# Storing a spectral layer's intermediates by even and odd frequency: fewer stores and loads, and some work moved

## The chip, the cores and the metric

The kernel runs on one core of a Trainium2 chip. Its time is the device time of one execution in microseconds (us), given as the median of several runs. A core has five engines that run side by side: TensorE (PE, matrix products), VectorE (DVE), ScalarE (ACT), GpSimd (POOL) and SyncE (SP). Here SP issues nearly all DMAs, the copies between DRAM and the core's memory. Each engine, and SP's issuing too, works through its own instructions in order; an instruction that has to wait holds back those behind it.

## The reference

The result is the sum of the input, a spectral filter of it, and a two-layer network on it:

```python
xn = layernorm(x)                      # x: 2048 x 512, rows normalised
A  = irfft2(rfft2(xn) * (w_r + 1j*w_i))   # over both axes
h  = xn @ w1 + b1                      # 512 -> 1792
B  = (h * tanh(softplus(h))) @ w2      # Mish, 1792 -> 512
return x + A + B
```

`x` is float32. Only 257 of the 512 columns of the spectrum are kept, since the input is real.

## The kernel before

All products run in float16 on TensorE. Each operand is split into a high and a low half, and a product is made of three matmuls (high by high, high by low, low by high), which gives nearly float32 accuracy. That makes `mm3`, lines 66 to 72, the commonest code on PE.

**The network.** The 2048 rows form four groups of 512 (`g`), the 1792 hidden columns 14 chunks of 128. `up(n)` makes one chunk of the hidden layer for one group (line 734, 12 matmuls of 128 x 512), `mish(n)`, `a_hi(n)` and `a_lo(n)` apply the activation and split it (ACT, ACT, DVE; lines 745, 754, 757), and `down(n)` adds the chunk's part to the output of its group (12 matmuls). Each `up` and each `down` is called a half tile. There are 56 of both, and they hardly depend on the spectral part, so they can be placed among its steps to keep PE busy.

**The spectral part.** The transform over the 2048 rows is done in two steps, as 128 x 16. In the first (`s1_mm`, `s1_mm_pair`), for each of 16 residues `s2`, the 128 rows of that residue are transformed. The result has 128 partitions: 64 first-axis frequencies by real and imaginary part. Residues of the last three groups are taken in pairs (`row_pair`): sums and differences of rows give even and odd frequencies apart, so that the partitions of such a tile come in the order all even, then all odd. For the first four residues the order is the natural one. `s1_out` copies the result out of the accumulator (ACT and DVE, lines 131 and 132) as float16 halves; `s1_store` or `s1_store_pair` writes it to the DRAM tensor `d_y1`. The latter spreads even and odd to alternate rows there, so `d_y1` has the natural order.

Then comes the second step, in four rounds `c` of 16 frequencies, each in four units: `load_yt` reads `d_y1` back with 128 partitions that mean something else (residue and slot), `p2_unit` transforms over the residues into the tile `z`, and `spectrum(c, par)` transforms over the columns (`dre` and `dim`, line 68), multiplies with the filter (DVE and POOL, with weights that `load_wx` brings: `wE`, `wO`) and splits the product into `u`. `par` is 0 for even columns, 1 for odd ones. A small detour for column 0 goes by two 2 KB DMAs (`er` and `es` to `g`) and back (`h` to `u`).

The way back mirrors this. `dp_unit` makes the inverse over the columns (`psA`, copied to `at`, lines 655 and 656), and four DMAs turn it to `ai` (line 662). `ip_pair` takes two units and makes the inverse over the residues (`psT`, line 678, copied to `tt`, lines 700 and 701) and stores it to the DRAM tensor `d_t` (line 707). There, too, even and odd frequencies are written apart, here as two halves of `d_t`. A pair has two tiles `tt`, each with two blocks of 64 partitions, each written as even and odd: eight stores. There are eight pairs. When all is stored, `load_yi` reads 16 tiles `yi` (line 865), each in two DMAs: even frequencies to partitions 0 to 63, odd to 64 to 127. Then `s1_inverse_pair` and `s1_inverse` make the last transform (`psY`), ACT copies it to `ys`, DVE adds it to the rows (`add_rows`, lines 896 to 898), and SP stores the output. The last sums of the network are added on DVE at line 844.

**What sets the order.** `opening` and `middle` are written out by hand and run as written: they hold the normalisation, the first transform of all rows, and the first 25 `up` and 20 `down`. `act_of(n)` is `up`, `mish`, `a_hi`, `a_lo`. `max_wm(c)` are reductions on DVE over the filter weights. After that the generator `stream_a` walks through the spectral steps and stops at each `yield`; at each stop the tuple `HALVES` says how many half tiles are put there: its first entry before the first `p2_unit`, its last ten before the ten inverse steps. Its entries add up to 67. There the framework's planner may still shift single instructions, but the first matmul of each step keeps its place in the order of the program. A few buffers tie the parts together: the two PSUM banks `ps_f` that all spectral products share, three buffers `q2` for `at` and `tt`, five buffers `big` for `yt`, `wE`, `wO` and others.

Of the kernel before, what the change touches and what calls it, by code (L numbers as in the profile page):

```python
# [11 lines left out]
F16 = mybir.dt.float16  # L12
# [7 lines left out]
P = 128  # L20
# [3 lines left out]
LAG = 2  # L24
LAST = 3
HALVES = (
# [4 lines left out]
)  # L31
NQ = 4
P2_AT, SP_AT = 0, 0
# [8 lines left out]
def spectral_mlp_kernel(ctx, tc, x, wt, w0, w1, b1, w2, cT, cIT, cM, out):  # L42
    nc = tc.nc
# [16 lines left out]
    outv = out.rearrange("(p s) d -> p s d", s=NS2)  # L60
    outw = out.rearrange("(h p s) d -> p s h d", h=2, s=NS2)

    d_y1 = dp.tile([64, P, 256], F16, tag="d_y1", name="d_y1")
    d_t = dp.tile([2, 2, 32, 2, 32, 256], F16, tag="d_t", name="d_t")

    def mm3(ps, stat, mov, start, stop, order=False):

# [20 lines left out]
    y1s = {}  # L88
# [46 lines left out]

    def s1_store(s2, n=2):
        k = s2 % 2 + 1
        nc.sync.dma_start(
            d_y1[4 * (s2 + 1 - n) : 4 * (s2 + 1)].rearrange("a p e -> p a e"),
            y1s[0][:, k - n : k].rearrange("p s a h e -> p (s a) (h e)"),  # L140
        )

    def s1_store_pair(s2):
        for t in range(2):
            nc.sync.dma_start(
                d_y1[4 * s2 : 4 * s2 + 8].rearrange("a (q t) e -> t q a e", t=2)[t],
                y1s[0][64 * t : 64 * t + 64].rearrange("p s a h e -> p (s a) (h e)"),
            )

    class Rows:  # L150
# [340 lines left out]
    def load_yt(c, b, n=1):  # L491
        t = big.tile([P, 2, 4, 2, P], F16, tag="big", name=f"yt_{c}_{b}")
        w = 2048 // n
        for k in range(n):
            o = (2 * c + b) * 2048 + k * w
            tc.keep_in_program_order(
                nc.sync.dma_start(
                    t.rearrange("p g a h e -> p (g a h e)")[:, k * w : (k + 1) * w],
                    d_y1.rearrange("a (c f) e -> (a c) (f e)", c=2)[:, o : o + w],
                )  # L500
            )
        yts.setdefault(c, []).extend([t[:, 0], t[:, 1]])
# [164 lines left out]
    def ip_pair(c, g):  # L667

        fgs = (4 * c + g, 4 * c + g + 1)
        ai = [ait.pop(fg) for fg in fgs]  # L670
        ps = [ps_f.tile([P, 4, P], F32, tag="f", name=f"psT_{fg}") for fg in fgs]
        tiles = [(u, r) for u in (1, 0) for r in (1, 0)]
        passes = ((0, 0), (0, 1), (1, 0))

        def quarter(u, r, k, v, ls):
            hc, hm = passes[k]
            qs = slice(64 * r, 64 * r + 64)
            return nc.tensor.matmul(  # L678
                ps[r][64 * u : 64 * u + 64, ls],
                c_ip2[qs, v, hc, :],  # L680
                ai[u][qs, ls, hm, :],
                start=k == 0,
                stop=k == 2,
            )

        def rest(k, u, r):
            return quarter(u, r, k, 0, slice(1 if fgs[u] == 0 else 0, 4))

        for k in range(3):
            for t in tiles:  # L690
                i = rest(k, *t)
                if (k, t) == (0, tiles[0]):
                    tc.keep_in_program_order(i)
        if fgs[0] == 0:
            for k in range(3):
                for r in range(2):
                    quarter(0, r, k, 1, slice(0, 1))
        for r in range(2):
            tt = tp.tile([P, 4, 2, P], F16, tag="q2", name=f"tt_{fgs[r]}", bufs=3)
            nc.scalar.mul(tt[:, :, 0, :], ps[r], 2.0**-12)  # L700
            nc.vector.scalar_tensor_tensor(  # L701
                tt[:, :, 1, :], ps[r], 2.0**-12, tt[:, :, 0, :], op0=ALU.mult, op1=ALU.subtract
            )
            for u in range(2):
                f = 2 * fgs[u]
                for t in range(2):
                    nc.sync.dma_start(  # L707
                        d_t[r, t, f : f + 2].rearrange("f c q e -> (c q) f e"),
                        tt[64 * u : 64 * u + 64].rearrange("p (f t) h e -> p t f (h e)", t=2)[:, t],
                    )  # L710


    macc, yacc = {}, {}
# [141 lines left out]
    def load_yi(todo):  # L855
        spots = []
        for tag in ("z", "u"):
            t = tp.tile([P, 4, 4, 2, P], F16, tag=tag, name=f"yi_{tag}")
            spots += [t[:, k] for k in range(4)]
        for k in range(4):  # L860
            t = tp.tile([P, 2, 4, 2, P], F16, tag=f"w{k}", name=f"yi_w{k}")
            spots += [t[:, 0], t[:, 1]]
        for s2, t in zip([4 * g + s + k for g, s, n in todo for k in range(n)], spots):
            for par in range(2):
                nc.sync.dma_start(
                    t[64 * par : 64 * par + 64].rearrange("p (r a) h e -> p r (a h e)", r=2),
                    d_t[:, par, :, :, 2 * s2 : 2 * s2 + 2].rearrange("r f c a e -> (f c) r (a e)"),
                )
            yis.append(t)

    def s1_inverse(g, s):
# [373 lines left out]
    def row_pair(r, j):  # L1245
        s2 = 4 * r.g + 2 * j
        ps = [s1_bank(s2 + k) for k in range(2)]
        s1_mm_pair(s2 // 2 - 2, r.eo[j], ps)
        for k in range(2):
            s1_out(s2 + k, ps[k])  # L1250
        s1_store_pair(s2)

    def act_of(n):
        up(n)
        mish(n)
        a_hi(n)
        a_lo(n)
# [5 lines left out]
    def middle(r, ps1):  # L1263
        load_ct(2)
        down(0)
        row_in(r, 0)
        x2 = load_rows(2)
        r.turn(0)
        s1_out(0, ps1[0])
        w2_part(2)  # L1270
        down(1)
        row_in(r, 1)
        r.turn(1)
        s1_out(1, ps1[1])
        s1_store(1)
        down(2)
        r.fold(0, FOLD)
        w2_part(3)
        down(3)
        row_in(r, 2)  # L1280
        r.turn(2)
        w2_part(4)
        down(4)
        row_in(r, 3)
        r.turn(3)
        down(5)
        row_pair(r, 0)
        r.fold(1, FOLD)
        w2_part(5)
        down(6)  # L1290
        q = Rows(2, x2)
        q.stats(0)
        q.stats(1)
        w2_part(6)
        down(7)
        q.stats(2)
        q.stats(3)
        down(8)
        r1, r = r, q
        nc.sync.dma_start(cMt, cM)  # L1300
        x3 = load_rows(3, "u")
        load_ct(3)
        act_of(14)
        row_pair(r1, 1)
        for s in range(4):
            r.aggr(s)
        r.root()
        down(9)
        load_res(0)
        row_in(r, 0)  # L1310
        r.turn(0)
        act_of(15)
        row_in(r, 1)
        r.turn(1)
        down(10)
        r.fold(0, FOLD)
        act_of(16)
        row_in(r, 2)
        r.turn(2)
        load_wm(0)  # L1320
        load_wm(1)
        down(11)
        row_in(r, 3)
        r.turn(3)
        act_of(17)
        row_pair(r, 0)
        load_wm(2)
        load_w0()
        down(12)
        r.fold(1, FOLD)  # L1330
        q = Rows(3, x3)
        for s in range(4):
            q.stats(s)
        act_of(18)
        load_wm(3)
        load_wm(4)
        down(13)
        mlp_end(0)
        r2, r = r, q
        homes[19] = tp.tile([P, 2, 512], F16, tag="q2", name="a_q2", bufs=3)  # L1340
        act_of(19)
        row_pair(r2, 1)
        for s in range(4):
            r.aggr(s)
        r.root()
        down(14)
        row_in(r, 0)
        r.turn(0)
        max_wm(0)
        act_of(20)  # L1350
        row_in(r, 1)
        r.turn(1)
        turn_w0()
        max_wm(1)
        down(15)
        r.fold(0, FOLD)
        load_wm(5)
        act_of(21)
        row_in(r, 2)
        r.turn(2)  # L1360
        down(16)
        row_in(r, 3)
        r.turn(3)
        load_wm(6)
        act_of(22)
        row_pair(r, 0)
        r.fold(1, FOLD)
        max_wm(2)
        down(17)
        max_wm(3)  # L1370
        load_wm(7)
        act_of(23)
        down(18)
        row_pair(r, 1)
        max_wm(4)
        max_wm(5)
        max_wm(8)
        act_of(24)
        max_wm(6)
        max_wm(7)  # L1380
        sum_wm()
        down(19)
        scale_wm()
        return 25, 20
# [28 lines left out]
def _dft_constants():  # L1413
# [8 lines left out]
    IT = T.reshape(128, 16, 128).transpose(2, 1, 0)  # L1422
    IT = IT.reshape(2, 32, 2, 16, 128).transpose(2, 1, 0, 3, 4).reshape(128, 16, 128)
    TW = T[:64, 4:].reshape(64, 6, 2, 2, 32, 2).transpose(2, 0, 1, 5, 3, 4).reshape(128, 6, 2, 64)
    T = T[:, :4].reshape(128, 4, 128)

    s = np.arange(16)
    a16 = 2 * np.pi * (np.outer(s, s) % 16) / 16
# [54 lines left out]

def _spectral_layout(wr, wi):

    f1 = np.arange(64)[:, None]
    j = _J[None]
    fp = np.where(f1 == 0, np.where(j < 8, 128 * j, 64 + 128 * (j - 8)), f1 + 128 * j)
    fm = (-fp) % 2048
# [51 lines left out]
```

## Time and profile before

| | us |
|---|---|
| median of 3 runs | 372.81 (371.75 to 373.81) |
| the profiled execution's own time | 371.67 |
| its span in the profile | 369.9 |
| PE busy | 355.4 |
| DVE busy | 279.6 |
| ACT busy | 188.6 |
| POOL busy | 48.3 |

The span runs from the first to the last recorded piece of work; the time of an execution has a little more around it. "Busy" is the time in which an engine has an instruction in work. Register, semaphore and DMA-issuing instructions do not count. Matmuls overlap: one of 128 x 512 is shown with 0.38 us while they follow one another every 0.22 us, so that busy times of single groups add up to more than the time they take. The rows of SP (`SPq`) show the issuing of a DMA; the transfer itself comes after, and its time to landing is listed apart. A row's value in brackets is the idle time of the engine just before it, with what ended the wait.

### The profile page before, as it was taken

Reading aid. Unit: us, or ns where it says so; the run is one execution under the profiler, and the core shown is the slowest. Engines: PE = TensorE matmul, PEld = TensorE weight load, DVE = VectorE, ACT = ScalarE, POOL = GpSimd, SP = SyncE. Lnnn points to the kernel's source line nnn. Section 1 sums busy time; section 2 is a strip of 40 time slices with the busy share of each in tenths; the row PEclk is TensorE's granted clock in tenths of the full one; section 3 lists DMA queues with packets and bytes.
Section 4 is the critical chain, followed back from the end, with each engine's and each line's share of the span. In section 5 each row is a group of like instructions: output and inputs, shape, how many; then the busy total and the mean of one; then the engine's idle time right before and its main releaser. Section 6 shows DMA issues by size and latency. Waiting matters only on the chain.

```text
span 369.9 us, 6245 instructions
## 1 busy us (share of the span) xinstructions
PE 355.4 (96%) x2283; PEld 174.3 (47%) x2283; DVE 279.6 (76%) x543; ACT 188.6 (51%) x288; POOL 48.3 (13%) x49
## 2 busy tenths in 40 slices
PE   7999999999999999999999999999989998979993
PEld 2544444444444445445554455445544543434453
DVE  4898998895788793789898747995399632249796
ACT  5989966545726623434446345445443543345421
POOL 0020002302206200302123003020212000000000
PEclk9999999999999999999999999999999999999998
DMA  8935944599786657048012536226833344466757
GB/s 274 316 126 189 217 110 92 117 225 250 178 252 148 164 132 277 2 114 289 12 30 64 128 60 207 65 80 138 244 82 100 66 103 96 89 183 202 186 121 221
DMA packets 61438, 54.98 MB, mean 149 GB/s; under 512 B 17456, under 2 KB 50512, under 8 KB 61280
## 3 DMA queue, kind: packets, MB, share of 16 engines
q1 hardware_dynamic: 60928, 54.06, 54.5%
q10 hardware_dynamic: 480, 0.52, 0.6%
q8 instruction: 18, 0.29, 0.3%
q14 instruction: 12, 0.10, 0.1%
HBM read 34.61 MB, written 12.58 MB: 128 GB/s over the span
## 4 chain that ended last, share of the span: by engine, by line
PE 73%; DVE 11%; DMA 6%; SPq 5%; ACT 2%; issue 2%; DVEq 0%; ACTq 0%
PE ph L734 33%; PE pa L68 10%; PE pa L72 10%; PE pa L71 10%; SPq L707 4%; DVE m L896 1%; DMA g<-es 1%; PE psS L108 1%; PE psT L678 1%; DVE at L656 1%; DMA ai<-at 1%; PE psP L522 1%; DMA x<-in_x_dram 1%; PE psP L532 1%; DMA g<-er 1%
## 5 line engine op out<-in xcount | busy, mean ns | idle before, releaser
L734 PE MATMUL ph<-xnT,w1t 128*128 128x512 f16 x672 | 153.6, 379 | 0.0
L734 PEld LDWEIGHTS <-w1t 128*128 128x128 f16 x672 | 64.7, 98 | 77.5 <-issue 2.5
L745 ACT ACTIVATE hb<-ph,b1t,fp_exp 128x512 f32<-128x512 f32 x56 | 43.2, 771 | 64.1 <-PE ph L734 64.1
L68 PE MATMUL pa<-w2t,a 128*128 128x512 f16 x181 | 68.7, 380 | 0.0
L72 PE MATMUL pa<-w2t,a 128*128 128x512 f16 x181 | 68.6, 379 | 0.0
L71 PE MATMUL pa<-w2t,a 128*128 128x512 f16 x181 | 68.6, 379 | 0.0
L757 DVE SCALAR_TENSOR_TENSOR a<-hb,ip_a,a 128x512 f16<-128x512 f32 x46 | 34.3, 748 | 31.5 <-ACT a L754 31.4
L754 ACT ACTIVATE a<-hb,ip_a 128x512 f16<-128x512 f32 x46 | 33.1, 720 | 2.3 <-DVE ip_a L294 1.2
L68 PEld LDWEIGHTS <-a 128*128 128x128 f16 x190 | 18.6, 98 | 21.3 <-issue 2.4
L72 PEld LDWEIGHTS <-a 128*128 128x128 f16 x190 | 18.6, 98 | 20.9
L71 PEld LDWEIGHTS <-a 128*128 128x128 f16 x190 | 18.6, 98 | 18.7
L255 POOL TENSOR_TENSOR xh<-xs,xh 128x512 f16<-128x512 f32 x12 | 15.4, 1294 | 56.7 <-ACT xh L229 37.4
L430 ACT ACTIVATE u<-w,sc_u 128x512 f16<-128x512 f32 x16 | 10.8, 715 | 18.0 <-DVE w L631 8.5
L701 DVE SCALAR_TENSOR_TENSOR tt<-psT,tt 128x512 f16<-128x512 f32 x16 | 10.5, 684 | 10.7 <-ACT tt L700 10.7
L537 DVE SCALAR_TENSOR_TENSOR z<-psP,z 128x512 f16<-128x512 f32 x16 | 10.8, 689 | 10.3 <-ACT z L536 10.3
L229 ACT ACTIVATE xh<-x,nb,rs 128x512 f16<-128x512 f32 x12 | 9.6, 805 | 12.2 <-DVE nb L223 7.3
L606 POOL TENSOR_TENSOR w<-X,wE 128x512 f32<-128x512 f32 x4 | 5.9, 1464 | 73.8 <-DMA wE<-in_wt_dram 45.6
L655 ACT ACTIVATE at<-psA 128x512 f16<-128x512 f32 x16 | 9.2, 588 | 11.3 <-PE psA L72 8.8
L700 ACT ACTIVATE tt<-psT 128x512 f16<-128x512 f32 x16 | 8.9, 587 | 11.8 <-PE psT L678 7.4
L162 DVE BATCH_NORM_STATS2 st<-x 128x6 f32<-128x512 f32 x16 | 10.3, 678 | 4.5 <-DMA x<-in_x_dram 4.5
L536 ACT ACTIVATE z<-psP 128x512 f16<-128x512 f32 x16 | 9.5, 595 | 7.1 <-PE psP L532 7.0
L431 DVE SCALAR_TENSOR_TENSOR u<-w,sc_u,u 128x512 f16<-128x512 f32 x16 | 11.3, 744 | 1.7 <-ACT u L430 1.7
(220 smaller groups left out, 578.2 us busy)
## 6 DMA issues: line engine op xcount, KB each, us to landing
wm<-in_wt_dram SPq DMA_DIRECT2D x8, 512.0 KB
ai<-at SPq DMA_DIRECT2D x64, 64.0 KB, 2.2
d_t<-tt SPq DMA_DIRECT2D x64, 64.0 KB, 2.1
w1s<-in_w_dram SPq DMA_DIRECT2D x7, 512.0 KB, 7.2
w2s<-in_w_dram SPq DMA_DIRECT2D x7, 512.0 KB, 3.2
x<-in_x_dram SPq DMA_DIRECT2D x12, 256.0 KB, 6.7
d_y<-y SPq DMA_DIRECT2D x12, 256.0 KB, 4.1
yt<-d_y SPq DMA_DIRECT2D x6, 512.0 KB
```

The costliest lines, as they stand in the source:

```text
L68: first = nc.tensor.matmul(ps, stat(0), mov(0), start=start, stop=False)
L71: nc.tensor.matmul(ps, stat(0), mov(1), start=False, stop=False)
L72: nc.tensor.matmul(ps, stat(1), mov(0), start=False, stop=stop)
L255: engine.tensor_sub(self.xh[s][:, 1, :], self.xs[s], self.xh[s][:, 0, :])
L430: nc.scalar.activation(dst_h, src, AF.Copy, scale=scale)
L431: nc.vector.scalar_tensor_tensor(dst_l, src, scale, dst_h, op0=ALU.mult, op1=ALU.subtract)
L537: nc.vector.scalar_tensor_tensor(zl, psv, 2.0**-14, zh, op0=ALU.mult, op1=ALU.subtract)
L707: nc.sync.dma_start(d_t[r, t, f : f + 2].rearrange("f c q e -> (c q) f e"), tt[64 * u : 64 * u + 64].rearrange("p (f t) h e -> p t f (h e) ...
L734: nc.tensor.matmul(ph[n + k], w1t[:, hw, dc, f * P : (f + 1) * P], xnT[g][:, hx, dc, :], start=(hw, hx, dc) == (0, 0, 0), stop=(hw, hx, dc ...
L745: nc.scalar.activation(hbt[n], ph.pop(n), AF.Mish, bias=b1t[:, f : f + 1], scale=s_exp[part_of(f)])
L754: nc.scalar.activation(act[n][:, 0, :], hbt[n], AF.Copy, scale=sc["a"])
L757: nc.vector.scalar_tensor_tensor(act[n][:, 1, :], hbt.pop(n), sc["a"], act[n][:, 0, :], op0=ALU.mult, op1=ALU.subtract)
```

## The change

The partition order "all even, then all odd" is now used for all tiles, from the first store to the last load:

- The constants for the first four residues (`T`) are permuted, so these tiles have it as well; the filter's layout (`f1` in `_spectral_layout`) is permuted to go with it.
- `d_y1` has even and odd frequencies as its outermost axis. Every store of `y` writes 64 partitions to 64 neighbouring rows. The first four residues take two stores for each two tiles, where they took one; the paired ones two, as before. `load_yt` reads one half or the other; pieces and sizes stay.
- In rounds 0 and 1 the second step now works on even frequencies, in rounds 2 and 3 on odd ones. So a block of 64 partitions of `tt` holds one kind only and is written by one store of 128 KB instead of two of 64 KB: four a pair instead of eight.
- A `yi` tile is loaded whole by one DMA of 256 KB instead of two of 128 KB.
- In `middle`, the last `row_pair` stands behind `act_of(24)` and `max_wm(4)` instead of ahead of them.
- `HALVES` has new entries, with the same number of them and the same sum.

The arithmetic, the number of matmuls and the bytes moved are the same.

```diff
 HALVES = (
-    2, 1, 0, 0, 1, 1, 1, 2, 0, 1, 1, 1, 2, 0, 0, 0, 0, 2, 0, 1, 0, 2, 0, 0, 1, 0, 1, 1, 0, 0, 1, 1,
-    0, 1, 1, 0, 0, 0, 0, 1, 0, 1, 0, 1, 0, 1, 1, 1, 1, 1, 0, 0, 0, 1, 0, 1, 1, 0, 0, 0, 0, 0, 1, 0,
-    0, 2, 0, 2, 0, 1, 1, 1, 0, 0, 1, 0, 1, 0, 0, 1, 1, 0, 0, 1, 1, 0, 0, 1, 1, 0, 4, 1, 1, 1, 3, 1,
-    2, 1, 1, 0,
+    3, 1, 0, 0, 0, 1, 0, 0, 0, 1, 1, 2, 1, 1, 2, 0, 1, 0, 2, 0, 0, 0, 0, 2, 1, 0, 1, 0, 1, 0, 0, 1,
+    2, 0, 1, 0, 0, 0, 0, 1, 1, 0, 2, 0, 0, 0, 1, 1, 0, 0, 0, 2, 0, 1, 1, 0, 1, 0, 0, 0, 0, 0, 1, 0,
+    1, 0, 1, 0, 2, 0, 2, 0, 1, 1, 1, 0, 0, 0, 1, 0, 2, 0, 0, 1, 1, 0, 1, 0, 0, 1, 3, 1, 1, 1, 1, 2,
+    2, 1, 1, 1,
 )
-    d_y1 = dp.tile([64, P, 256], F16, tag="d_y1", name="d_y1")
-    d_t = dp.tile([2, 2, 32, 2, 32, 256], F16, tag="d_t", name="d_t")
+    d_y1 = dp.tile([2, 64, 2, 32, 256], F16, tag="d_y1", name="d_y1")
+    d_t = dp.tile([2, 64, 2, 32, 256], F16, tag="d_t", name="d_t")
...
     def s1_store(s2, n=2):
         k = s2 % 2 + 1
-        nc.sync.dma_start(
-            d_y1[4 * (s2 + 1 - n) : 4 * (s2 + 1)].rearrange("a p e -> p a e"),
-            y1s[0][:, k - n : k].rearrange("p s a h e -> p (s a) (h e)"),
-        )
-
-    def s1_store_pair(s2):
         for t in range(2):
             nc.sync.dma_start(
-                d_y1[4 * s2 : 4 * s2 + 8].rearrange("a (q t) e -> t q a e", t=2)[t],
-                y1s[0][64 * t : 64 * t + 64].rearrange("p s a h e -> p (s a) (h e)"),
+                d_y1[t, 4 * (s2 + 1 - n) : 4 * (s2 + 1)].rearrange("a c q e -> (c q) a e"),
+                y1s[0][64 * t : 64 * t + 64, k - n : k].rearrange("p s a h e -> p (s a) (h e)"),
             )
...
-            o = (2 * c + b) * 2048 + k * w
+            o = (2 * c + b) % 4 * 2048 + k * w
...
-                    d_y1.rearrange("a (c f) e -> (a c) (f e)", c=2)[:, o : o + w],
+                    d_y1[(2 * c + b) // 4].rearrange("a c q e -> (a c) (q e)")[:, o : o + w],
...
             for u in range(2):
-                f = 2 * fgs[u]
-                for t in range(2):
-                    nc.sync.dma_start(
-                        d_t[r, t, f : f + 2].rearrange("f c q e -> (c q) f e"),
-                        tt[64 * u : 64 * u + 64].rearrange("p (f t) h e -> p t f (h e)", t=2)[:, t],
-                    )
+                f = 4 * fgs[u]
+                nc.sync.dma_start(
+                    d_t[r, f : f + 4].rearrange("f c q e -> (c q) f e"),
+                    tt[64 * u : 64 * u + 64].rearrange("p f h e -> p f (h e)"),
+                )
...
-            for par in range(2):
-                nc.sync.dma_start(
-                    t[64 * par : 64 * par + 64].rearrange("p (r a) h e -> p r (a h e)", r=2),
-                    d_t[:, par, :, :, 2 * s2 : 2 * s2 + 2].rearrange("r f c a e -> (f c) r (a e)"),
-                )
+            nc.sync.dma_start(
+                t.rearrange("p (r a) h e -> p r (a h e)", r=2),
+                d_t[:, :, :, 2 * s2 : 2 * s2 + 2].rearrange("r f c a e -> (f c) r (a e)"),
+            )
...
     def row_pair(r, j):
...
-        s1_store_pair(s2)
+        s1_store(s2 + 1)
...
         down(18)
+        max_wm(4)
+        act_of(24)
         row_pair(r, 1)
-        max_wm(4)
         max_wm(5)
         max_wm(8)
-        act_of(24)
         max_wm(6)
...
-    T = T[:, :4].reshape(128, 4, 128)
+    T = T[:, :4].reshape(128, 4, 2, 32, 2).transpose(0, 1, 4, 2, 3).reshape(128, 4, 128)
...
-    f1 = np.arange(64)[:, None]
+    f1 = np.arange(64).reshape(32, 2).T.reshape(64, 1)
```

## The prediction

> **What bounds the kernel now.** I read first the busy time by stretch, to see where TensorE (PE) is not full, since PE work is the same before and after. Columns: stretch, its length, busy us (count) of PE, weight loads, VectorE (DVE), ScalarE (ACT), POOL, PE clock, DMA share, GB/s.
>
> ```profile
> 0.00:20.00 20.00, 17.51 (x103) 8.97 (x104) 13.96 (x35) 15.48 (x24) 2.04 (x9) 1.00 0.86 278
> 20.00:230.00 210.00, 210.00 (x1285) 101.85 (x1283) 170.88 (x335) 116.05 (x177) 37.65 (x34) 1.00 0.56 148
> 230.00:240.00 10.00, 9.21 (x53) 4.46 (x51) 9.59 (x20) 4.75 (x8) 0.05 (x1) 1.00 0.22 61
> 270.00:280.00 10.00, 8.37 (x48) 4.03 (x46) 9.81 (x19) 4.02 (x6) 0.00 (x0) 1.00 0.25 65
> 290.00:330.00 40.00, 36.22 (x244) 17.36 (x243) 12.19 (x19) 15.67 (x24) 0.00 (x0) 1.00 0.44 102
> 360.00:369.90 9.90, 4.12 (x43) 3.34 (x41) 6.25 (x15) 1.37 (x2) 0.00 (x0) 0.87 0.75 219
> ```
>
> PE is full from 20 to 230 us. What a change of the spectral part can win is 0.79 us (230 to 240), 1.63 (270 to 280) and 3.78 (290 to 330), together 6.20, and some of the last 9.9 us. The clock is 1.00 in all of it. The waits of PE name what it lacked:
>
> ```profile
> PE psY L108 <- DMA yi_z<-d_t: 2.2, 3, 1.3
> PE dim L68 <- DVE at L656: 1.4, 2, 0.8
> PE psT L678 <- DMA ai<-at: 1.1, 1, 1.1
> ```
>
> Two of the three are DMAs issued by SP (SyncE). SP's own order of work shows why they are late (start, us, what):
>
> ```profile
> 305.74 5.10 SPq L662 DMA_DIRECT2D ai<-at  x8
> 310.94 10.71 SPq L707 DMA_DIRECT2D d_t<-tt  x16
> 322.57 5.27 SPq L865 DMA_DIRECT2D yi_z<-d_t  x8
> ```
>
> From 305.74 to 327.84 SP issues without a pause: 32 DMAs, 0.65 to 0.67 us apart. DMA engines are at a 0.44 share over 290 to 330. So the number of issues, not bytes, sets this stretch: `ai` of the last pair leaves behind stores of an earlier one, and sixteen stores stand before the first load of the inverse transform.
>
> **The change, part by part.** *Issue count.* The price of an issue against its size, and issue to landing:
>
> ```profile
> L707 SPq DMA_DIRECT2D d_t<-tt x64: 574/605/1652, 206.1 to 321.0; - x64
> L145 SPq DMA_DIRECT2D d_y<-y x12: 581/621/1352, 72.0 to 133.5; - x12
> d_t<-tt SPq DMA_DIRECT2D x64, 64.0 KB, 2.1
> d_y<-y SPq DMA_DIRECT2D x12, 256.0 KB, 4.1
> yi_z<-d_t SPq DMA_DIRECT2D x8, 128.0 KB, 2.9
> yt<-d_y SPq DMA_DIRECT2D x4, 256.0 KB, 4.5
> ```
>
> A 64 KB store takes 605 ns to issue and a 256 KB one 621: size costs SP nothing. The `d_t` stores go from 64 of 64 KB to 32 of 128 KB (four a pair), the `yi` loads from 32 of 128 KB to 16 of 256 KB; the stores of the first four `y` tiles go from 2 to 4. At 0.65 us that takes 20.8 + 10.4 off SP and adds 1.3 near 44 and 63 us, where PE is full (20 to 230): zero, at most 1.3 if that cover went. Pieces stay 512 B for stores and 1 KB a row for `yi`. Landing is not shown for the new shapes: a 128 KB store lies between 2.1 and 4.1, I take 2.8 (nearer the smaller one by size); a 256 KB load of full rows lies between 2.9 and 4.5, I take 3.5. The `yt` loads keep size and piece; their rows only lie closer in DRAM: zero, hidden by the same full stretch.
>
> *The end of the spectral part (290 to 330).* Rows for the last pair, and the length of one half tile of PE cover (12 matmuls):
>
> ```profile
> 312.57 0.75 PE L678 MATMUL psT<-ai,cMt 64*64 64x512 f16 x8 [1.12 <-DMA ai<-at]
> 314.21 0.69 DVE L701 SCALAR_TENSOR_TENSOR tt<-psT,tt 128x512 f16<-128x512 f32 x1 [2.94 <-ACT tt L700]
> 327.61 0.81 PE L108 MATMUL psY<-yi_z,cITt 64*64 64x256 f16 x21 [0.40 <-DMA yi_z<-d_t]
> 240.29 2.59 PE ph L734 x12
> ```
>
> Before, from the end of `psT` (about 313.5) to the inverse getting its data (327.61) go 14.1 us. New: first `tt` half ready 1.4 later (314.21 + 0.69), its two stores until 2.7, two more until 4.0. The last is issued at 3.4, lands at 3.4 + 2.8 = 6.2; two `yi` loads, the second issued at 6.85, landed at 6.85 + 3.5 = 10.4. HALVES now leaves four half tiles between this `psT` and the first inverse instead of five: 4 x 2.59 = 10.4 us of PE work. The stall is thus about nil, 2.3 at the slow ends (3.4 + 4.1 + 0.65 + 4.5 = 12.65) and nil at the fast ones; I take 0.5. The eight stores of the pair before are now four, so `ai` leaves 2.6 us earlier, and the 1.12 goes. The other 0.5 of this stretch I leave with 0.3. Gain: 3.78 - 0.8 = 3.0, between 1.0 and 3.8.
>
> By the Trainium skill, SBUF — State Buffer, section on Door 1, a transfer on partitions 0 to 63 reaches 8 of 16 ports, and one on 128 reaches all; with its fixed 2 us and 27 GB/s a port (an estimate from that page) the 128 KB store and the full-row 256 KB load each land in 2.6 us. The stall would be nil by it and the gain 0.5 more. The 4.1 of the 256 KB store above is slower than the 3.2 that it would give, so the rows stay in the sum.
>
> *The middle (230 to 280).* Here PE waited for DVE to empty its banks, and DVE for DMAs:
>
> ```profile
> 228.69 0.42 DVE L578 TENSOR_TENSOR r<-g,c0t 4x256 f32<-4x256 f32 x1 [1.26 <-DMA g<-es]
> 257.14 5.17 SPq L707 DMA_DIRECT2D d_t<-tt  x8
> 262.36 0.59 SPq L506 DMA_DIRECT2D wE<-in_wt_dram  x1
> 263.54 0.67 SPq L572 DMA_DIRECT2D g<-es  x1
> 266.24 0.69 DVE L605 TENSOR_TENSOR w<-X,wE 128x512 f32<-128x512 f32 x1 [1.98 <-DMA wE<-in_wt_dram]
> ```
>
> Near 262 the `wE` load and the small `g` transfers stand directly behind eight stores; with four, they leave up to 2.6 earlier, more than the 1.63 that PE lost after. Near 221 it is the same eight stores, then three 512 KB loads, then `g`: with the loads gone earlier the 1.26 shrinks, and with it the 0.79. Against that, HALVES is rearranged. Adding up its entries, the count is equal again at the same points (4 at the first spectrum, 19 at the second half of the second, 25, 30, 34, 36, 41 after), but between them it differs: the two halves of the first spectrum have one half tile between them instead of four, those of the second five instead of six.
>
> ```profile
> 182.90:196.90 14.00, 14.00 (x102) 7.75 (x100) 13.67 (x25) 7.50 (x13) 2.94 (x2) 1.00 0.14 39
> ```
>
> In the second spectrum DVE was busy 13.67 of 14.0 us with PE just covered. One half less bares at most 2.59; as the first spectrum now gives DVE its work earlier, I take 0.5, and 0.6 in all other places. Gain: 2.42 - 1.1 = 1.3, between -1.0 and 2.4.
>
> *The moved pair (front).* The last `row_pair` goes behind one `act_of` and one `max_wm`, and HALVES starts with 3 for 2, so four half tiles still stand between its `psS` and the first use of `yt`.
>
> ```profile
> 130.07 0.85 PE L108 MATMUL psS<-eo,cTt 64*64 64x256 f16 x24
> 131.59 1.29 DVE L132 SCALAR_TENSOR_TENSOR y<-psS,y 128x512 f16<-128x512 f32 x2 [0.60 <-ACT y L131]
> 137.25 1.76 SPq L497 DMA_DIRECT2D yt<-d_y  x4
> 141.39 0.22 PE L522 MATMUL psP<-cMt,yt 128*128 128x128 f16 x1
> L745 ACT ACTIVATE hb<-ph,b1t,fp_exp 128x512 f32<-128x512 f32 x56 | 43.2, 771 | 64.1 <-PE ph L734 64.1
> L757 DVE SCALAR_TENSOR_TENSOR a<-hb,ip_a,a 128x512 f16<-128x512 f32 x46 | 34.3, 748 | 31.5 <-ACT a L754 31.4
> ```
>
> But its copies now queue behind that tile's Mish, cast and rest on ACT and DVE (771 ns, about as much again, 748), which start only where `psS` starts: DVE gets to `y` about 1.6 us after `psS` ends instead of 0.7, so its two stores, and the `yt` loads that wait behind them on SP, go about 1.0 later. The first loads left at 137.25 and their data was read near 141.3 with PE full, so the slack is unknown: the cost is between 0 and 1.5, I take 0.5, the middle.
>
> *The tail.* The last ten inverses come earlier among the half tiles (after 60, 62, 64 of them instead of 62, 63, 65).
>
> ```profile
> 329.70:366.40 36.70, 34.41 (x289) 18.11 (x287) 34.17 (x70) 13.35 (x20) 0.00 (x0) 1.00 0.68 185
> 363.90 0.22 PE L72 MATMUL pe<-w2t,a 128*128 128x128 f16 x1
> 365.98 0.34 DVE L844 SCALAR_TENSOR_TENSOR y<-pe,s_out,y 128x128 f32<-128x128 f32 x1
> ```
>
> DVE ends 2.2 us after PE, having been idle 2.5 of 36.7 us; fed earlier it can make up to 1.7 of that, but may also hold PE if inverses come faster than it adds them (six pairs). I take 0.5, between -0.5 and 1.7.
>
> *Sum.* 3.0 + 1.3 - 0.5 + 0.5 = 4.3 us. The profiled execution took 371.67 (span 369.9 and 1.77 around it): 367.4. The median of the runs, 372.81, lies 1.14 above it, so the forecast is 372.81 - 4.3 = 368.5.
>
> **The rivals.** *Issues are not what binds, bytes are:* all bytes stay, and fewer, larger transfers land later. The Trainium skill, DMA: Bandwidth & Descriptors, section Issuing engines are not separate DMA queues, speaks for this: issue time is "usually small relative to the DMA itself". Against it: the 0.65 us spacing whatever the size, and the 0.44 share. Then the end keeps its 3.78 and only the slow-landing bounds apply: gain 1.3 - 0.5 = 0.8, 372.0. Chance 0.18.
>
> *DVE becomes the bound of the last stretch:* 34.17 us of DVE work cannot begin before the first inverse and ends 2 us behind PE; if five pairs one half tile apart back up on DVE and hold the two banks of the next, the tail gives nothing and 1.5 of the end's gain goes back: 4.3 - 0.5 - 1.5 = 2.3, 370.5. For it: 34.17 of 36.7. Against: PE's remaining work is as long, and `ys` has two buffers. Chance 0.14.
>
> *Slower: the first spectrum's missing cover.* With one half tile instead of four between its halves, `dre` of the second needs banks that DVE must empty first. If DVE does that only behind the whole of the first half's work, the three missing half tiles are bared, 3 x 2.59 = 7.8; less the 4.3 it makes 372.81 + 3.5 = 376.3. It decides from 4.3 us bared on. For it: DVE is full in this part (13.67 of 14.0). Against: the emptying subtractions come first in the code, and the half tiles are returned after. Chance 0.08.
>
> **How the numbers follow.** Forecast 0.60, the rivals 0.18, 0.14, 0.08. About 0.5% (1.86 us) can be told from no change: faster is below 370.95, slower above 374.67. Forecast and the DVE rival lie below: 0.74; bytes: 0.18 same; cover: 0.08 slower. The terms' good ends together give 3.8 + 2.4 + 1.7 = 7.9, hardly all at once; I end the range at a gain of 6.8 (366.0), and above at 372.6, which takes in the bytes rival.
>
> **What would show it.** In the changed profile: 32 `d_t` stores and 16 `yi` loads at 0.6 us each; SP with pauses between 295 and 325; PE idle in the 40 us before the first inverse down from 3.78 to about 0.8; waits for `ai` gone; DVE not waiting for `wE` and `g` in the last two spectra; DVE's last instruction under 2 us behind PE's. The forecast is wrong if issue time grows with the store's size, if new idle time of PE stands between 140 and 230, or if the first `psP` waits for `yt` by more than 1.5.

## The result, and the profile after

| | before | changed |
|---|---|---|
| median, us | 373.23 (4 runs, 371.75 to 373.81) | 363.52 (4 runs, 363.37 to 363.65) |
| profiled execution's own time | 371.67 | 363.37 |
| its span | 369.9 | 361.6 |

The ratio is 0.9746, with a 95% interval of 0.9715 to 0.9776: 9.7 us faster. The forecast was 4.3, the fastest end of its range 366.0. The direction was right; the gain is more than double what was forecast and outside the range.

Busy time by stretch in the changed kernel (columns as before: stretch, length, PE, weight loads, DVE, ACT, POOL, PE clock, DMA share, GB/s):

```profile
0.00:20.00 20.00, 17.43 (x103) 8.93 (x104) 14.01 (x35) 15.53 (x24) 2.04 (x9) 1.00 0.87 278
20.00:230.00 210.00, 209.66 (x1274) 101.42 (x1273) 170.71 (x337) 115.20 (x176) 37.36 (x34) 1.00 0.58 148
230.00:240.00 10.00, 10.00 (x71) 5.27 (x73) 9.60 (x20) 5.15 (x9) 0.94 (x1) 1.00 0.19 54
270.00:280.00 10.00, 10.00 (x48) 4.58 (x47) 8.86 (x18) 3.19 (x5) 2.37 (x2) 1.00 0.17 47
290.00:330.00 40.00, 40.00 (x295) 18.70 (x293) 17.78 (x30) 18.60 (x29) 0.00 (x0) 1.00 0.61 163
```

PE is full from 230 to 330. All three holes of the kernel before (0.79, 1.63 and 3.78 us) are closed, and one of 0.34 is new, before 230. All waits of PE that are left, in its waits:

```profile
PE ps_w L1010 <- POOL eps L1034: 1.3, 1, 1.3
PE pt L257 <- ACT xh L184: 1.2, 2, 0.9
PE psP L516 <- DVE z L531: 0.3, 1, 0.3
```

The first two belong to the first 20 us. None is for a DMA. SP's order of work in the last spectral stretch now has pauses (start, us, what):

```profile
301.19 5.59 SPq L656 DMA_DIRECT2D ai<-at  x8
307.82 6.85 SPq L700 DMA_DIRECT2D d_t<-tt  x8
316.61 1.92 SPq L857 DMA_DIRECT2D yi_z<-d_t  x4
```

Before, 32 issues stood without a pause between 305.7 and 327.8. Now there is a pause of a microsecond before the stores and of about 2 before the first load, which waits for the last store to land.

**How much each stall was.** The 6.20 us that the prediction set as the most to be won between 230 and 330 is too little, because of how busy time is counted. Two neighbouring matmuls of the kernel before, from PE's timeline:

```profile
235.73 0.38 PE L72 MATMUL dre<-z,cMt 128*128 128x512 f16 x1
236.90 0.38 PE L68 MATMUL dim<-z,cMt 128*128 128x512 f16 x1 [0.79 <-DVE at L656]
```

They start 1.17 us apart, where undisturbed ones follow at 0.22: the stall cost 0.95, and the profile shows 0.79, since a matmul shown with 0.38 us still covers 0.16 of the hole behind it. Counted from start to start, the eight stalls of the kernel before come to 7.7 us: 2.9 in the middle (near 236 and 276) and 4.8 at the end (300 to 328). In the changed kernel 0.5 is left, so 7.2 us of stalls are gone. PE's last matmul starts at 356.61, before at 363.90: 7.3 earlier, which the stalls thus account for. From there to the end of the span go 5.0 us instead of 6.0. Together that is the 8.3 us between the two profiled executions (371.67 and 363.37). The other 1.4 us between the medians come from executions of the kernel before that were slower than its profiled one; `fill` below bears on the cause.

### The profile page after: what moved, and what is told of

Same layout as the page of the kernel before. It is cut to its first block, busy times and chain, and to the rows that moved or that the text cites. A ratio compares the mean times of both kernels' runs of the same rounds, so it can differ in the third digit from the quotient of the medians.

```text
span 361.6 us, 6167 instructions
## 1 busy us (share of the span) xinstructions
PE 353.9 (98%) x2283; PEld 174.0 (48%) x2283; DVE 278.5 (77%) x543; ACT 187.7 (52%) x288; POOL 47.8 (13%) x49
## 4 chain that ended last, share of the span: by engine, by line
PE 90%; DVE 6%; ACT 1%; DMA 1%; issue 0%; DVEq 0%
PE ph L727 39%; PE pa L68 13%; PE pa L71 12%; PE pa L72 12%; PE psT L672 2%; PE psS L108 1%; PE psY L108 1%; DMA x<-in_x_dram 1%; PE psA L68 1%; PE psA L71 1%; PE psA L72 1%; PE psP L516 1%; PE psP L526 1%; DVE u L425 1%; PE psP L519 1%; DVE xh L188 1%
## 5 line engine op out<-in xcount | busy, mean ns | idle before, releaser
L695 DVE SCALAR_TENSOR_TENSOR tt<-psT,tt 128x512 f16<-128x512 f32 x16 | 10.4, 683 | 7.3 <-ACT tt L694 7.3
L600 POOL TENSOR_TENSOR w<-X,wE 128x512 f32<-128x512 f32 x4 | 5.1, 1274 | 69.6 <-DVE X L593 69.6
L694 ACT ACTIVATE tt<-psT 128x512 f16<-128x512 f32 x16 | 8.8, 589 | 10.7 <-PE psT L672 8.8
```

Of the source, the lines that this page charges most:

```text
L695: nc.vector.scalar_tensor_tensor(tt[:, :, 1, :], ps[r], 2.0**-12, tt[:, :, 0, :], op0=ALU.mult, op1=ALU.subtract)
```

## The experiments

The theory was that SP's issues were what PE waited for ("issues"): removing 48 of them won the time, and the half tiles only had to go where the room was. The rivals were that the new places of the half tiles won it ("placing"), or that bytes and landings count, not the number of transfers ("bytes"). The runs were made in three groups, each with its own runs of the kernel before, to which the ratios refer: a median of 372.8 for `layout_only`, `sched_only`, `stores8` and `loads2`, 373.1 for `pool_queue`, `fill`, `after_unmoved` and `tail0`, 372.74 for `mid8`, `end8`, `end2` and `end2_tail0`.

**The layout alone.** `HALVES` and the place of `row_pair` go back to the old ones.

```diff
 HALVES = (
-    3, 1, 0, 0, 0, 1, ...
+    2, 1, 0, 0, 1, 1, ...
...
         down(18)
+        row_pair(r, 1)
         max_wm(4)
-        act_of(24)
-        row_pair(r, 1)
         max_wm(5)
         max_wm(8)
+        act_of(24)
```

> The changed kernel with HALVES and the place of the last row_pair as before: only the new layout, with 32 stores and 16 loads. Theory 'issues' (what was won is SP's issue time; the half tiles only had to be put where it leaves room): most of the 9.7 us, 365 to 368. Rival 'placing' (the half tiles' new places won it, whatever SP does): at most 2 us, 371 to 373.

Measured: 364.74 us (364.17 to 364.81), ratio 0.9778 (0.974 to 0.9817). So the layout wins 8.1 us, even with half tiles that were placed for the old one. "Placing" alone is out. PE keeps one wait in the spectral part:

```profile
PE psA L68 <- DVE tt L695: 0.6, 1, 0.6
```

The new places bring another 1.2: PE's last matmul starts 0.6 earlier than here (357.19 against 356.61), and the rest of the span behind it is 5.0 instead of 5.7.

**The places alone.** The kernel before with the new `HALVES` and the moved pair.

```diff
 HALVES = (
-    2, 1, 0, 0, 1, 1, ...
+    3, 1, 0, 0, 0, 1, ...
...
         down(18)
+        max_wm(4)
+        act_of(24)
         row_pair(r, 1)
-        max_wm(4)
         max_wm(5)
         max_wm(8)
-        act_of(24)
```

> The kernel before with the new HALVES and the moved row_pair: 64 stores and 32 loads as before. 'Issues': SP still issues without a pause from 300 to the first inverse, which now has four half tiles of cover instead of five, so a stall of PE of some 4 us or more there: 372 to 376. 'Placing': 364 to 367.

Measured: 370.9 us (370.5 to 372.12), ratio 0.9949 (0.9926 to 0.9971). Neither expectation was right: it is 1.9 faster, not slower. The stalls at the end did grow as "issues" had it, by 1.1 us in these two waits together:

```profile
PE psY L108 <- DMA yi_z<-d_t: 2.6, 2, 1.3
PE psT L678 <- DMA ai<-at: 1.8, 1, 1.8
```

But the waits for DVE in the middle shrank from 2.4 to 0.6, with all 64 stores still there, the 0.5 for `tt` is gone, and the stretch behind PE's last matmul went from 6.0 to 4.9; together that is more. So the middle's stalls have two cures: the layout alone ends them (`layout_only` shows none), and the new places alone end most of them.

**Eight stores again, same bytes.** In the changed kernel each 128 KB store of `d_t` is cut in two; the partitions, the pieces and the loads stay.

```diff
-                f = 4 * fgs[u]
-                nc.sync.dma_start(d_t[r, f : f + 4]..., tt[64 * u : 64 * u + 64]...)
+                for t in range(2):
+                    f = 4 * fgs[u] + 2 * t
+                    nc.sync.dma_start(d_t[r, f : f + 2]..., tt[64 * u : 64 * u + 64, 2 * t : 2 * t + 2]...)
```

> The changed kernel with every 128 KB store of d_t cut into two of 64 KB on the same 64 partitions: eight stores a pair, same bytes and same pieces, loads whole. 'Issues': PE idle before the first inverse returns, eight issues of 0.65 more stand on its way, 5 us less what is slack: 366 to 370. 'Bytes' (fewer transfers do not matter, the bytes do): 363.5 as the changed kernel.

Measured: 369.57 us (368.08 to 370.86), ratio 0.9908 (0.9876 to 0.9939): 6.0 of the 9.7 us are gone, with the same bytes, layout and order. "Bytes" is out. SP again issues sixteen stores in a row, and the first load leaves at 321.80, in the changed kernel at 316.61:

```profile
309.47 10.77 SPq L701 DMA_DIRECT2D d_t<-tt  x16
321.80 1.93 SPq L858 DMA_DIRECT2D yi_z<-d_t  x4
```

PE's waits at the end are back, and one of those in the middle:

```profile
PE psY L108 <- DMA yi_z<-d_t: 2.4, 2, 2.0
PE psT L672 <- DMA ai<-at: 0.9, 1, 0.9
PE dre L68 <- DVE at L650: 0.7, 1, 0.7
```

This run also showed something that no theory had. Its busy time by stretch after the stall:

```profile
322.00:324.00 2.00, 0.55 (x3) 0.05 (x1) 0.00 (x0) 1.38 (x2) 0.00 (x0) 1.00 0.54 157
324.00:326.00 2.00, 1.02 (x23) 0.80 (x24) 0.75 (x1) 0.12 (x1) 0.00 (x0) 0.92 0.87 270
326.00:328.00 2.00, 2.00 (x12) 0.58 (x5) 0.32 (x1) 1.26 (x2) 0.00 (x0) 0.50 0.98 284
328.00:330.00 2.00, 2.00 (x8) 0.84 (x7) 1.97 (x4) 0.00 (x0) 0.00 (x0) 0.73 1.07 354
```

After idle stretches of 2.0 and 0.4 us PE's granted clock (the third column from the right) falls to 0.50 for more than 2 us, and matmuls start 0.43 us apart instead of 0.22. It doesn't seem to happen each time. Of the seven executions of this kernel three have a mean clock of 0.998 or 0.999 and take 368.1 to 368.4; four, the profiled one (0.993) among them, have 0.992 or 0.993 and take 369.6 to 370.9. If the mean clock tells the fall in those without a profile, it costs about 2 us. The profile of `sched_only`, also at 0.993, has it too, behind idle stretches of 1.3 and 1.3 us:

```profile
328.00:330.00 2.00, 2.00 (x11) 0.80 (x7) 0.04 (x1) 1.26 (x2) 0.00 (x0) 0.50 0.70 206
```

The Trainium skill (TensorE: Matmul & The Clock Gate, Part 1) says that the clock goes to half after at least one idle window of about 3.4 us, and that the windows run freely, so that the moment of a change depends on where in a window the work falls. The half speed and the chance in it agree. But here 2.4 us of waiting, broken by one matmul, were enough, and the measurement decides. (Behind the wait came 23 small matmuls of 64 x 64 before the large ones; whether those count as work for the clock no run shows.)

**Loads in two.** The changed kernel with each `yi` load cut into two of 64 partitions.

```diff
-            nc.sync.dma_start(t..., d_t[:, :, :, 2 * s2 : 2 * s2 + 2]...)
+            for par in range(2):
+                nc.sync.dma_start(t[64 * par : 64 * par + 64]..., d_t[:, 32 * par : 32 * par + 32, :, ...]...)
```

> The changed kernel with every yi load cut into two of 64 partitions: 32 loads. 'Issues': only the first pair of inverses waits, for four issues instead of two, 1.3 us later less what is slack (the profile of the changed kernel shows no wait there): 363.5 to 365. Were the loads' landing what counts, 128 KB landing sooner than 256 KB would make it no slower or faster.

Measured: 363.67 us (363.37 to 364.07), ratio 0.9754 (0.9715 to 0.9792): no difference that can be told from the changed kernel. The 16 saved loads are hidden; the stores carry the gain.

**POOL as second issuer.** The kernel before, in its old layout; every second `d_t` store of the last three pairs is issued by POOL, which has no other work there.

```diff
                 for t in range(2):
-                    nc.sync.dma_start(
+                    queue = nc.gpsimd if t and fgs[0] >= 10 else nc.sync
+                    queue.dma_start(
                         d_t[r, t, f : f + 2]...
```

> The kernel before, with every second d_t store of the last three pairs issued by POOL instead of SP: same stores, same sizes, same loads, 12 issues fewer on SP from 285 us on. 'Issues': SP reaches the first yi load some 5 us earlier and most of PE's 3.8 us (4.5 with what the modelled ends hide) before the first inverse go, and the drop of the clock with them: 367 to 369. 'Bytes': 372 to 373, as before.

Measured: 368.51 us (367.88 to 368.66), ratio 0.9873 (0.9827 to 0.9919). Twelve issues moved to another engine win 4.6 us, with no byte, size or half tile changed. PE's waits:

```profile
PE dim L68 <- DVE at L656: 1.1, 2, 0.6
PE dre L68 <- DVE at L656: 0.8, 1, 0.8
PE psA L68 <- DVE tt L701: 0.5, 1, 0.5
PE psT L678 <- DMA ai<-at: 0.3, 1, 0.3
```

The 2.2 us for `yi` are gone; the waits of the middle, where SP still issues eight stores a pair, remain. SP's last two pairs now take 6.5 us instead of 10.7, and the first load leaves at 318.12 instead of 322.57:

```profile
308.86 6.54 SPq L708 DMA_DIRECT2D d_t<-tt  x8
318.12 5.41 SPq L866 DMA_DIRECT2D yi_z<-d_t  x8
```

The number and the size of the transfers are as before, so at the end neither of them is the cause, but that they stand in one row on SP. POOL's stores also have a queue of their own (0.79 MB in 384 packets) and land in 2.3 us, SP's in 2.1, so they don't win by landing faster. That the issuing itself takes the time is seen in SP's rows of `stores8`, where all stores keep their queue: sixteen issues in 10.77 us.

**Middle and end apart.** The changed kernel with eight stores for the first five pairs only (`mid8`) or for the last three only (`end8`).

```diff
-                f = 4 * fgs[u]
-                nc.sync.dma_start(d_t[r, f : f + 4]..., ...)
+                w = 2 if fgs[0] < 10 else 4      # end8: fgs[0] >= 10
+                for t in range(0, 4, w):
+                    f = 4 * fgs[u] + t
+                    nc.sync.dma_start(d_t[r, f : f + w]..., ...)
```

> The changed kernel with eight 64 KB stores for the first five pairs and four of 128 KB for the last three. By the gaps between PE's matmul starts in the kernel before, the middle holds 2.9 us: 364.5 to 366.5, with PE waiting for DVE near 236 and 276. By the prediction's term 1.3 (what it took to be won in the middle): 364.3 to 365.

> The opposite: four stores for the first five pairs, eight for the last three. By the gaps the end holds 4.9 us, and a fall of PE's clock in some executions: 367 to 370, and wider apart than the changed kernel's. By the prediction's term 3.0: 366 to 367. mid8 and end8 together should lose what stores8 lost, 6.0 us.

Measured: `mid8` 365.73 us (365.38 to 368.06), 2.2 above the changed kernel; `end8` 368.3 us (367.15 to 369.12), 4.8 above. Together that is 7.0, a little more than the 6.0 of `stores8`. The size of `end8` is that of the gaps between matmul starts (4.8), not the prediction's term (3.0). `mid8` doesn't size the middle: of its waits only 0.7 is there, one for DVE near 236, as in `stores8`, where the kernel before has three of 2.4 together. The larger one, 1.2, is at the first inverse, behind pairs that are stored as in the changed kernel. It was not expected: the loads left 0.5 later after `psT` than in the changed kernel, and the second one's data came later too; why is open. It says that the cover at the first inverse has little to spare. `end8` waits only at the end. First `mid8`, then `end8`:

```profile
PE psY L108 <- DMA yi_z<-d_t: 1.2, 1, 1.2
PE dre L68 <- DVE at L650: 0.7, 1, 0.7
```

```profile
PE psT L672 <- DMA ai<-at: 2.0, 1, 2.0
PE psY L108 <- DMA yi_z<-d_t: 1.8, 2, 1.4
```

**Filling the hole.** The kernel before with 14 matmuls that nobody reads, ahead of the first inverse.

```diff
         next(plan)
+        if n == 0:
+            ps = ps_h.tile([P, 512], F32, tag="h", name="ps_fill")
+            for k in range(14):
+                i = nc.tensor.matmul(ps, w1t[:, 0, 0, :P], w1t[:, 0, 0, :512], start=True, stop=True)
...
```

> The kernel before with 14 matmuls that nobody reads (3.0 us) put on PE just ahead of the first inverse, where PE stood idle for 2.8 us; they are work left over, not part of the computation. Theory 'clock': in the executions of the kernel before that take about 2 us more than its profiled one, PE's clock drops to half after that idle time, as the profile of stores8 shows; with PE kept busy no execution drops, so all lie within 0.6 us of 371.9, and the median falls by about 1 us. Rival: the spread of the kernel before comes from the DMAs; then the spread of 3 us stays and the time rises by up to 0.3.

Measured: 372.29 us (371.5 to 374.21, 12 executions) beside 373.1 (371.72 to 377.19, 17 executions); ratio 0.9972 (0.9944 to 1.0001). The slowest executions are gone and the median is 0.8 lower, but the interval just holds 1, and the spread of 2.7 us is not the 0.6 that "clock" alone asks for. The profiled one took 373.36 at a mean clock of 0.997, and shows why:

```profile
PE dre L68 <- DVE at L656: 1.7, 1, 1.7
PE psT L678 <- DMA ai<-at: 1.5, 1, 1.5
```

In the profile of the kernel before these were 1.0 and 1.1. So two things widen the spread of the kernel before: stalls that last longer or shorter from one execution to the next, and the clock that sometimes falls. The mean clocks of the executions help to part them. Of the 17 of the kernel before, 11 have a mean clock under 0.995, as the two profiles with a fall have, and a median of 373.9; the other six have 372.3. With the hole filled only one of 12 is under 0.995, and the median is 372.3, that of the six. This fits a fall of the clock that costs the median about 0.8 us, and stalls that vary as the rest. It is not proof: a single profile of the kernel before was taken, and it has no fall at the first inverse. The changed kernel shows neither: its clock is 0.998 to 1.0, and its four executions lie within 0.3 us.

**The move of the pair alone.** The changed kernel with the last `row_pair` back ahead of `act_of(24)`.

```diff
         down(18)
+        row_pair(r, 1)
         max_wm(4)
-        act_of(24)
-        row_pair(r, 1)
         max_wm(5)
         max_wm(8)
+        act_of(24)
```

> The changed kernel with the last row_pair back ahead of act_of(24); HALVES as changed. If the move itself does not matter (the changed profile shows no wait of psP for yt), 363.5 within 0.4. If the move brought what placing won, about 364.7 as layout_only.

Measured: 363.71 us (363.41 to 363.89), ratio 0.9747 (0.9701 to 0.9792). The move is worth nothing that can be measured.

**The tail.** Three small edits to the changed kernel: the last inverse earlier (`tail0`), the last tile finished in two pieces instead of three (`end2`), and both.

```diff
-    2, 1, 1, 1,        # tail0: last entry of HALVES
+    2, 1, 1, 0,
...
-        for o, w in ((0, 256), (256, 128), (384, 128)) if s == 3 else ((0, D),):    # end2
+        for o, w in ((0, 256), (256, 256)) if s == 3 else ((0, D),):
...
-            pool, tag = (ps_f, "f") if o == 384 else (ps_h, "h")
+            pool, tag = (ps_f, "f") if o == 256 else (ps_h, "h")
```

> The changed kernel with the last entry of HALVES 0 instead of 1: the last inverse comes ahead of end_of(2). If DVE's order alone sets the end (it finishes 1.1 us after PE), 362.9 to 363.5; if PE's idle banks or DVE's sum of work set it, 363.5 within 0.3.

> The changed kernel with the last tile finished in two pieces of 256 columns instead of 256, 128, 128: one output store fewer on SP and on ACT at the very end, where SP still issues 1.1 us after DVE's last sum, but a longer last sum. 363.0 to 363.6.

> The same with the last inverse ahead of end_of(2) (as in tail0), so that only the two pieces' sums and stores are left after PE: 362.8 to 363.4 if SP's issues at the end are what is left of the tail, 363.6 as tail0 if not.

Measured: `tail0` 363.6 us (363.42 to 363.83), `end2` 362.85 (362.73 to 362.95), both together 363.01 (362.93 to 363.17). The end of the changed kernel, from its timeline:

```profile
356.61 0.22 PE L72 MATMUL pe<-w2t,a 128*128 128x128 f16 x1
357.26 0.60 DVE L837 SCALAR_TENSOR_TENSOR y<-pe,s_out,y 128x128 f32<-128x128 f32 x2
357.90 1.14 SPq L782 DMA_DIRECT2D out_dram<-y  x2
```

DVE is done at 357.86, and SP then still issues two stores for 1.14 us. Finishing in two pieces, with one store fewer on SP, is worth 0.7: `end2` is the fastest of all versions, and its executions don't overlap with those of the changed kernel. The order of DVE's sums (`tail0`) is worth nothing.

## Why the prediction was right or wrong

**Issues bind, not bytes: right.** `stores8` and `pool_queue` show it from both sides, for the end; in the middle `sched_only` shows that new places for the half tiles do nearly as much as fewer issues. The price of a store held: 605 ns for 64 KB before, 616 for 128 KB now, from the changed kernel's line of stores and, second, its line of loads:

```profile
L700 SPq DMA_DIRECT2D d_t<-tt x32: 574/616/635, 206.4 to 314.1; - x32
L857 SPq DMA_DIRECT2D yi_z<-d_t x4: 386/464/469, 316.6 to 318.1; - x4
```

The first four whole-row loads were even cheaper to issue than the 0.65 taken. Landings, from its list of DMA issues:

```profile
d_t<-tt SPq DMA_DIRECT2D x32, 128.0 KB, 2.5
yi_z<-d_t SPq DMA_DIRECT2D x4, 256.0 KB, 4.9
```

The 128 KB store took 2.5 against 2.8 taken. The estimate of 2.6 from the Trainium skill (SBUF — State Buffer, Door 1 and The DMA setup-cost knee) came nearer here. For the load the list's 4.9 is far above that estimate, and above the 3.5 taken, in a burst of 16 loads in which the DMA share rises to 1.0. But the sum needs only the first two loads, and their data was there at 320.29, at most 3.7 us after the first was issued (316.61).

**The end, 3.0 forecast: mis-sized, 4.8.** The chain was right in sum: from the end of `psT` (309.89) to the first inverse (320.29) go 10.4 us, as worked out, and four half tiles (4 x 2.59) cover it:

```profile
309.05 0.84 PE L672 MATMUL psT<-ai,cMt 64*64 64x512 f16 x12
311.39 1.28 DVE L695 SCALAR_TENSOR_TENSOR tt<-psT,tt 128x512 f16<-128x512 f32 x2
320.29 0.85 PE L108 MATMUL psY<-yi_z,cITt 64*64 64x256 f16 x24
```

Its steps were each a little off: the first copy starts 1.5 after `psT` ends, where the prediction had it done at 1.4; the first load leaves at 6.7 instead of 6.2; and the data was there in time all the same. What failed is the deduction: 0.5 for a stall and 0.3 for the rest were taken off, and none came; and 1.0 us were hidden in the way busy time is counted.

**The middle, 1.3 forecast: mis-sized, 2.4, and a second cause left out.** The stalls of 2.9 us are gone, and 0.5 came for the rearranged half tiles, where 1.1 were taken off. The 0.5 is in one place: `psP` near 177, after the first spectrum, not in the second. The mechanism told is there: DVE's waits for `wE` and `g`, 4.3 us in three waits between 220 and 280 before, don't appear in the changed profile. But the prediction counted the rearranged half tiles only as a loss, and `sched_only` shows that by themselves, with eight stores a pair, they bring the waits of the middle from 2.4 to 0.6. What each does of the 2.9 can't be parted, since either is nearly enough.

**The front, 0.5 lost: wrong, nothing.** DVE gets to `y` 1.5 us after `psS` ends (at about 133.4), as forecast, and the stores leave 0.8 later, counted from the start of `psS`. But the `yt` loads behind them don't: they leave 7.0 us after that start, before 7.2 (130.07 to 137.25), because from the end of the second store's issue they wait 2.1 us and not 3.1. Why the stores land sooner no run shows. The first `psP` doesn't wait. First the kernel before, then the changed one:

```profile
132.90 1.26 SPq L145 DMA_DIRECT2D d_y<-y  x2
```

```profile
132.60 0.85 PE L108 MATMUL psS<-eo,cTt 64*64 64x256 f16 x24
134.95 1.28 DVE L132 SCALAR_TENSOR_TENSOR y<-psS,y 128x512 f16<-128x512 f32 x2
136.26 1.26 SPq L139 DMA_DIRECT2D d_y<-y  x2
139.59 1.76 SPq L491 DMA_DIRECT2D yt<-d_y  x4
143.76 0.22 PE L68 MATMUL psP<-cMt,yt 128*128 128x128 f16 x1
```

**The tail, 0.5 forecast: 1.0.** The stretch behind PE's last matmul went from 6.0 to 5.0. `layout_only`, with 5.7, and `sched_only`, with 4.9, show that most of it is the new `HALVES`.

The four terms, as measured, are 4.8 + 2.4 + 0 + 1.0 = 8.2 us, where 4.3 were forecast; the profiles lie 8.3 apart.

**The step from the profile to the median: wrong in kind.** The prediction subtracted its gain, read from the profiled execution, from a median 1.14 us above it, as if the changed kernel would have that distance too. It went with the stalls (363.52 and 363.37 now). It also read the clock as 1.00 throughout; its own last row, from 360 on, has 0.87, and other executions of the kernel before have mean clocks down to 0.988. That stalls vary and sometimes bring the clock down fits this, as `fill` shows, but how much each did is not settled. This 1.4 us and the 1.5 us hidden in the busy times are why even the range was too slow: its best case, 7.9 us, rested on the idle time as shown, in one execution of 371.67.

**The rivals.** "Bytes" (0.18) fell with `stores8` and `pool_queue`. One issue of 0.6 us is short beside a landing of 2.5, but sixteen in a row ahead of the first load are not. "DVE becomes the bound" (0.14) didn't come in the form told: PE never waited for banks there. The missing cover of the first spectrum (0.08) cost the 0.5 us named above, not 7.8.

## What to carry to other kernels

Where PE waits for DMAs at a low DMA share, count the issues on the queue: at 0.6 us for each store here, from 64 to 256 KB, fewer and larger stores, or a second issuing engine, won the time without a byte less. Where half tiles are moved at the same time, run each change alone: in the middle either was nearly enough. Add up stalls by the starts of matmuls, not by busy time, and treat a spread of the runs as part of what a stall costs. Where the cover has been counted and comes out even, as it did here, a further deduction for a stall needs a reason of its own.

## What the runs showed of the hardware

- Idle stretches of 2.0 and 0.4 us on PE, with one matmul between, brought its granted clock to 0.50 in the profile of `stores8`, and 1.3 and 1.3 us in that of `sched_only`; by the mean clocks it happened in four of seven executions of `stores8`, which took about 2 us more, nearly as much again as the stall.
- Behind a matmul of 128 x 512, an idle time of PE is shown 0.16 us shorter than it costs (0.79 shown, 0.95 between the starts).
- Issuing a load of 256 KB to 128 partitions in 1 KB pieces took 464 ns (the first four `yi` loads of the changed kernel; all 16 lie between 360 and 825), one of 128 KB to 64 partitions 605 ns (the kernel before).
- In a burst of such 256 KB loads the landings rose from 4.9 us (`yi_z`) to 6.9 (`yi_w`), at a DMA share of up to 1.1 (changed kernel).
